# Softmax sums of the first five head pairs: GpSimd adds three key tiles to three others before TensorE sums them, and the written order is planned anew

## The chip, the cores and the metric

The kernel runs on one core of one Trainium2 chip. The metric is the device time of one launch in microseconds; three runs of the kernel before gave 902.53, 903.97 and 904.75 us, a median of 903.97.

## The reference

```python
q_pool = q.reshape(B, H, S // 2, 2, D).mean(axis=3)      # B=4, H=8, S=1152, D=64
scores = scale * q_pool @ k.T                            # 576 queries by 1152 keys, a head
attn = exp(scores - max(scores))
attn = attn / (sum(attn) + 1e-9)                         # the sum over 1152 keys
x = heads side by side (attn @ v)                        # 2304 tokens by 512
h = x @ w_in                                             # 512 by 2048
out = (h * clip(h + 3, 0, 6) / 6) @ w_out                # 2048 by 512
```

All data are float32.

## The kernel before, in words

Attention goes by 16 head pairs g, numbered batch by batch. The scores are kept transposed: keys on the 128 partitions (nine key tiles t), queries on the free axis, 288 of the 576 at a time (halves h = 0, 1). So a unit of work (g, h) holds two heads j, nine tiles each of 128x288, in one tile `s`. For each unit TensorE makes the score tiles (`scores`, step `mm`), ScalarE copies them to `s` (`keep`, step `cp`) and VectorE keeps a running maximum over the tiles (`most`, step `mx`). `fold`, `best` and `spread` (steps `s1` to `s3`) turn it into one maximum for each query, spread over the partitions. `lessen` (step `su`, L470) subtracts it from three key tiles at a time (128x864), on VectorE or, in the first part, on GpSimd (which then reads a copy `mb` that ScalarE makes of it). `expo` (step `ex`, L478) takes the exponential, again three tiles at a time. `values` (step `av`, L495) multiplies with V.

The denominators are made in two ways. The first five pairs (g below EARLY = 5, "the first part") use `sums_of_four` (step `o4`, L525 to L531): for each of nine key tiles and two heads a matmul with a stationary block of ones (32 columns), into four 32-row strips of one PSUM tile, 18 matmuls in a unit, each recorded as two instructions. `keep_sums` (`sc`) and `pick_sums` (`de`) then reduce the strips. The other eleven pairs ("late" in the code) use `total` (step `ad`, L480 to L488): GpSimd adds three key tiles to three others (n = 0), adds the last three (n = 1) and folds the three that are left (n = 2, 3) in a tile `d` of pool `dp`, which has two buffers.

Also in the first part the two weight matrices are converted (`load_raw`, `convert`, `save_w`): raw words are loaded in 32 pieces of 512 KB, go in seven steps through ScalarE, GpSimd and VectorE (the last one, step 6, L629, on GpSimd or VectorE) and are written back to DRAM. A step named `second` waits for all maxima of the first five pairs and for 24 of the conversions; then PSUM is divided anew. Only after it do the late pairs' scores start, and the gated MLP (`do_layer` L183, `do_project` L216), which goes over chunks of 256 tokens between the attention steps. The last 768 tokens come in a loop of their own after attention.

The order of the instructions on each engine is written out by `Order.run`, a list scheduler on the host: every step has a place (a number, smaller goes first), costs for each engine that may run it, steps that it needs, and buffers that it takes and frees. Whenever an engine is free in the plan, it takes the ready step with the smallest place; a third number in a cost is added to the place for that engine (BIAS). Places come from the constants at the top: PER (distance between pairs, in the first part and later), AT and ATL (offsets of the steps of a pair, early and late), START and SLOPE (the MLP's chunks), LAG and MLP (steps inside a chunk), CONV and CSTEP (conversions). The engines run the list in order, so an instruction that waits holds up what stands behind it on its engine. The steps of the change are `o4` (L791), `ad` (L767 to L771), and the constants of L22 to L33.

Of the kernel before, what the change touches and what calls it, by code (L numbers as in the profile page):

```python
# [18 lines left out]


SBUFS = 3
START = (94.79, 128.23, 169.33, 204.1, 247.91, 270.62)  # L22
SLOPE = (2.19, 3.02, 2.72, 2.51, 1.78, 3.47)
LAG, MLP = 9.42, (2.56, -1.5, 4.75, 1.71)
CONV, CSTEP = 27.2, (39.17, 25.6)
NEAR = 5
EARLY, FCV = 5, 12
CVB = 1
BIAS = (-3.16, 165.7, 1.3, -2.73, 8.4, 2.65)
CUT = 8  # L30
PER = (18.24, 19.02)
AT = (1.82, 3.28, -1.17, 8.45, 1.17, 16.24, 17.65, 6.2, 8.03, -0.11, 4.3, 2.83, -21.04, 27.48)
ATL = (0.23, 5.42, -4.41, 15.94, 13.8, 18.37, 11.77, 34.99, -2.44, 15.27, 4.54, 6.0, -6.43, -6.01)  # L33
TAIL = 768


class Order:
# [9 lines left out]
    def add(self, key, place, cost, fn, needs=(), takes=(), frees=()):  # L47
        assert key not in self.key, key
        self.key[key] = len(self.steps)
        self.steps.append((place, cost, fn, tuple(needs), tuple(takes), tuple(frees)))  # L50
# [76 lines left out]
def pooled_attention_then_gated_mlp(ctx, tc, q, k, v, w_in, w_out, out):  # L127
    nc = tc.nc
    B, H, S, D = q.shape
    DM, DFF = w_in.shape  # L130
    P = 128
    KT = S // P
    KC = 3
# [70 lines left out]
    def hidden(pool, ps, xs, w, n):  # L204
        layer(ps, xs, w)
        r6 = relu(pool, ps, n)
        gate(r6, r6, ps)
        gh = upper(pool, r6, n)
        return gh, lower(pool, r6, gh, n)
# [46 lines left out]
    with ExitStack() as a:  # L256
# [12 lines left out]
        HQ = SQ // NH  # L269
        TQ = QT // NH  # L270
        ones = const.tile([P, 32], F32, name="ones")
# [12 lines left out]
        ps_t, s_t, m_t, st_t, d_t, av_t, x_t, xo_t, q_t = {}, {}, {}, {}, {}, {}, {}, {}, {}  # L284
# [40 lines left out]
        def bank(g):  # L325
            return ("v",) if g < NEAR else ("s",)
# [197 lines left out]

        def sums_of_four(eng, g, h):  # L525
            ps = d_t["p", g, h] = ps_av.tile([P, 512], F32, tag="av", name="psr")
            for t in range(KT):
                for i in (t % 2, 2 + t % 2):
                    nc.tensor.matmul(
                        ps[32 * i:32 * (i + 1), 0:HQ], ones[:, 0:32], s_t[g, h][:, i // 2, t, :], start=(t < 2), stop=(t > KT - 3)  # L530
                    )  # L531

        def keep_sums(eng, g, h):
            d_t["s", g, h] = sm.tile([P, HQ], F32, tag="sc", name="sc", bufs=1)
# [147 lines left out]
        add = od.add  # L682
        MOVE = {"ACT": (360, 440), "DVE": (480, 555, 1.5)}

        def place(g):
            return PER[0] * min(g, EARLY) + PER[1] * max(g - EARLY, 0)


        for g in range(NG):
            lead = place(g - 1)  # L690
            at = ATL if g >= EARLY else AT
            UNIT = PER[g >= EARLY] / 4
            early = g == 0
# [7 lines left out]
            late = g >= EARLY  # L701
            for c in C3 if late else range(2):
                n = 3 if late or c else 6
# [3 lines left out]
                cost = (750, 855) if late else (90 + 92 * n, 190 + 92 * n)  # L707
                add(("kh", g, c), z + 2 + c, {"ACT": cost} if late else {"ACT": cost, "DVE": (68 + 133 * n, 150 + 133 * n, BIAS[2])},
                    partial(keep_k, g=g, c=c),
# [3 lines left out]
            for h in range(NH if late else 1):  # L713
                z = place(g) + 2 * UNIT * h - at[1]
                for j in range(2 if late else 1):
# [3 lines left out]
                        [("pq", g, 1)] + [("second",)] * (g == NEAR) + before, bank(g), ("qp",) if h == NH - 1 and end or not late else ())  # L719
                    add(("qh", g, h, j), z, {"ACT": (300, 400)} if late else {"ACT": (505, 605), "DVE": (668, 750, BIAS[3])}, partial(keep_q, g=g, h=h, j=j),  # L720
                        [("tq", g, h, j)], () if j else ("q",), () if late else bank(g))
                    if late:
                        add(("ql", g, h, j), z, {"DVE": (375, 450)}, partial(keep_q, g=g, h=h, j=j), [("qh", g, h, j)], (), bank(g))
            for h in range(NH):
                for j in range(2):
# [36 lines left out]
                    for c in C3:  # L762
                        add(("su", u, c), z + at[3] + c, {"DVE": (970, 1045)} if late else {"DVE": (970, 1045), "POOL": (2000, 2050, BIAS[0])}, partial(lessen, u=u, c=c),
                            [("s3", u) if late else ("sb", u)] + ([("su", u, c - 1)] if c and late else []), (),
                            (("st",) if c == 2 else ()) if late else (("st", u, 3), ("mb", u, 3)))
                        add(("ex", u, c), z + at[3] + 1 + c, {"ACT": (831, 930)}, partial(expo, u=u, c=c), [("su", u, c)])
                    for n in range(4 if late else 0):  # L767
                        cost = 2000 if n < 2 else 765
                        add(("ad", u, n), z + at[4] + 1.5 * n, {"POOL": (cost, cost + 50)}, partial(total, u=u, n=n),
                            [("ex", u, c) for c in (range(2) if n == 0 else (2,) if n == 1 else ())] + ([("ad", u, n - 1)] if n else []),  # L770
                            () if n else ("d",), (("S", u[:2], 3),) if n == 1 else ())  # L771
# [5 lines left out]
                n = len(cuts) - 2  # L777
# [6 lines left out]
                ya = y + n  # L784
                z += at[6]
                add(("ev", g, h), ya, {"ACT": (296, 376), "DVE": (370, 450, BIAS[4])}, partial(take_v, g=g, h=h), [("av", g, h, n)], ("x",), ("av",))
                if late:
                    add(("de", g, h), z, {"PE": (510, 730)}, partial(sums, g=g, h=h),
                        [("dj", (g, h, j)) for j in range(2)] + [("av", g, h, n)], ("av",), ("dh",))
                else:  # L790
                    add(("o4", g, h), ya, {"PE": (2700, 2900)}, partial(sums_of_four, g=g, h=h), [("av", g, h, n)], ("av",), ("S",))  # L791
                    add(("sc", g, h), ya, {"ACT": (300, 400)}, partial(keep_sums, g=g, h=h), [("o4", g, h)])
                    add(("de", g, h), ya, {"PE": (510, 730)}, partial(pick_sums, g=g, h=h), [("sc", g, h)])
                add(("rc", g, h), z, {"DVE": (200, 280)}, partial(recip, g=g, h=h), [("de", g, h)])
                add(("rw", g, h), z, {"ACT": (370, 450), "POOL": (980, 1000, BIAS[5])}, partial(widen, g=g, h=h), [("rc", g, h)])
                add(("qu", g, h), z, {"PE": (250, 470)}, partial(quotient, g=g, h=h), [("rw", g, h)])
# [5 lines left out]
        COSTS = ({"ACT": (580, 680)}, {"POOL": (660, 670)}, {"DVE": (500, 570)}, {"DVE": (630, 700)}, {"DVE": (630, 700)},  # L802
                 {"POOL": (690, 720), "ACT": (600, 700, 3)}, {"POOL": (1280, 1300), "DVE": (640, 720, BIAS[1])})
        for f in range(NFC):
# [20 lines left out]
        for m in range(NFC * len(chunks)):  # L825
            c, f = divmod(m, NFC)
            z = START[c] + SLOPE[c] * f
            if f == 0:
# [37 lines left out]
    with ExitStack() as a:  # L866
# [11 lines left out]
        for step in range(NFC + lag):  # L878
            for n, f in ((0, step), (1, step - lag)):
                if 0 <= f < NFC:  # L880
                    w = parts[n][1]
                    g = hidden(gt if n else gp, ph[n].tile([P, DM], F32, tag="h", name="ph")[:, 0:w], xs[n], w_t[f, 0], w)
                    pend.append((n, g, f))
                    if len(pend) > 2:
                        n, g, f = pend.pop(0)
# [36 lines left out]
```

## Time and profile before

| | |
|---|---|
| median of three runs | 903.97 us |
| the profiled execution's own time | 904.39 us |
| its span, first to last instruction | 902.5 us |
| TensorE (PE) busy | 863.0 us, 96% |
| VectorE (DVE) busy | 638.4 us, 71% |
| ScalarE (ACT) busy | 618.4 us, 69% |
| GpSimd (POOL) busy | 523.4 us, 58% |
| mean granted TensorE clock | 0.987 |

The shares are averages over two stages that differ. Until about 185 us the first five pairs and the conversions run; from about 260 us on, TensorE has hardly a gap. Rows of windows (busy time of every engine in a stretch) show that better than the totals. A timeline row gives start, duration, engine, line, operation, operands and count, and in brackets the idle time of that engine before it with what ended it.

### The profile page before, as it was taken

The numbers are of one execution on the slowest core, as the hardware profiler recorded it, in microseconds if no ns is written. First come the engines' busy times: TensorE is split into PE (matmuls) and PEld (weight loads), VectorE is DVE, ScalarE is ACT, GpSimd is POOL, SyncE is SP. The second block draws the span as 40 slices with busy tenths as digits, with TensorE's granted clock in tenths as the row PEclk, the third lists the DMA queues.
The fourth block names the chain that finished last, engine by engine and source line by source line (L and its number), as shares of the span: only waits on it lengthen the run. The fifth ranks groups of instructions, "written<-read, shape, count | busy, mean of one in ns | idle before, by whom it ended". The sixth has DMA issues, their size and how long they took to land.

```text
span 902.5 us, 16987 instructions
## 1 busy us (share of the span) xinstructions
PE 863.0 (96%) x5976; PEld 671.9 (74%) x5976; DVE 638.4 (71%) x1196; ACT 618.4 (69%) x1320; POOL 523.4 (58%) x474
## 2 busy tenths in 40 slices
PE   4889989989999999999999999999999999999997
PEld 3445445457778887889888888888888877888886
DVE  5879989887898888777877777787876761322222
ACT  4878888875778888878777787787876763222222
POOL 2556747444567888867686977677885695000000
PEclk9889999999999999999999999999999999999999
DMA  9978576469988777769686787787678658534433
GB/s 261 277 225 257 201 232 218 156 205 303 323 273 276 222 234 207 245 218 320 213 246 214 223 280 236 266 273 250 221 262 273 198 189 282 181 121 135 138 96 93
DMA packets 113396, 204.00 MB, mean 226 GB/s; under 512 B 44448, under 2 KB 68000, under 8 KB 113312
## 3 DMA queue, kind: packets, MB, share of 16 engines
q1 hardware_dynamic: 112624, 201.55, 70.1%
q10 hardware_dynamic: 688, 1.38, 0.5%
q8 instruction: 47, 0.77, 0.4%
q14 instruction: 37, 0.30, 0.1%
HBM read 171.97 MB, written 30.93 MB: 225 GB/s over the span
## 4 chain that ended last, share of the span: by engine, by line
PE 75%; DMA 7%; DVE 7%; ACT 5%; issue 3%; POOL 2%; SPq 0%; DVEq 0%; ACTq 0%; POOLq 0%
PE ph L183 21%; PE po L216 16%; PE pav L495 12%; PE pqk L408 12%; PE pt L216 5%; DVE m L426 3%; DMA raw<-in_moe_w_in_dram 2%; DMA raw<-in_moe_w_out_dram 2%; PE pst L465 2%; ACT s L310 2%; PE pt L382 1%; DMA qr<-in_q_dram 1%; ACT s L478 1%; DMA w_d<-scratch 1%; PE psr L521 1%
## 5 line engine op out<-in xcount | busy, mean ns | idle before, releaser
L470 DVE TENSOR_TENSOR s<-s,pst 128x864 f32<-128x864 f32 x168 | 173.8, 1047 | 32.6 <-PE pst L465 27.4
L478 ACT ACTIVATE s<-s 128x864 f32<-128x864 f32 x192 | 176.7, 933 | 24.6 <-DVE s L470 22.6
L183 PE MATMUL ph<-mxmxh,w 128*128 128x256 f32 x896 | 181.0, 285 | 0.0
L426 DVE TENSOR_TENSOR m<-pqk,m 128x288 f32<-128x288 f32 x308 | 139.6, 453 | 38.2 <-ACT s L310 27.0
L495 PE MATMUL pav<-s,vr 128*64 128x288 f32 x1152 | 156.6, 417 | 0.0
L310 ACT COPY s<-pqk 128x288 f32<-128x288 f32 x396 | 145.9, 400 | 14.3 <-PE pqk L408 10.8
L183 PEld LDWEIGHTS ph<-mxmxh,w 128*128 128x128 f32 x896 | 146.5, 190 | 2.2 <-issue 0.9
L216 PE MATMUL po<-w,gh 128*128 128x512 f32 x448 | 139.3, 392 | 0.0
L188 ACT ACTIVATE r<-ph,three 128x256 f32<-128x256 f32 (+1 forms) x128 | 64.1, 501 | 102.1 <-PE ph L183 98.2
L183 PE MATMUL ph<-mxmxl,w 128*128 128x256 f32 x448 | 126.4, 282 | 0.0
L408 PE MATMUL pqk<-qh,kT 128*128 128x288 f32 x396 | 124.2, 327 | 2.2 <-DVE m L426 1.0
L488 POOL TENSOR_TENSOR d<-s 128x864 f32<-128x864 f32 x44 | 90.1, 2048 | 58.1 <-ACT s L478 55.2
L495 PEld LDWEIGHTS pav<-s,vr 128*64 128x64 f32 x1152 | 78.1, 138 | 59.1 <-issue 11.1
L192 DVE SCALAR_TENSOR_TENSOR r<-r,ph 128x256 f32<-128x256 f32 (+1 forms) x128 | 57.5, 449 | 90.2 <-ACT r L188 89.7
L408 PE MATMUL pqk<-ql,kT 128*128 128x288 f32 x396 | 111.6, 294 | 0.0
L201 POOL TENSOR_TENSOR gl<-r,gh 128x256 fp32r<-128x256 f32 x96 | 70.9, 738 | 52.1 <-ACT gh L196 34.1
L216 PEld LDWEIGHTS po<-w,gh 128*128 128x128 f32 x448 | 84.3, 188 | 14.5
L216 PE MATMUL po<-w,gl 128*128 128x512 f32 x224 | 90.0, 402 | 1.5 <-DMA w<-w_d 1.5
L488 POOL TENSOR_TENSOR d<-d,s 128x864 f32<-128x864 f32 x44 | 90.3, 2051 | 0.6
L408 PEld LDWEIGHTS pqk<-qh,kT 128*128 128x128 f32 x396 | 74.6, 188 | 17.8 <-DVE m L426 5.2
L183 PEld LDWEIGHTS ph<-mxmxl,w 128*128 128x128 f32 x448 | 85.2, 190 | 0.8
L196 ACT CAST gh<-r 128x256 fp32r<-128x256 f32 (+1 forms) x128 | 55.7, 435 | 39.3 <-DVE r L192 26.7
(97 smaller groups left out, 1500.7 us busy)
## 6 DMA issues: line engine op xcount, KB each, us to landing
w<-w_d SPq DMA_DIRECT2D x224, 512.0 KB, 5.0
w_d<-scratch SPq DMA_DIRECT2D x32, 512.0 KB, 5.5
kr<-in_k_dram SPq DMA_DIRECT2D x32, 288.0 KB, 5.0
vr<-in_v_dram SPq DMA_DIRECT2D x16, 576.0 KB, 4.0
qr<-in_q_dram SPq DMA_DIRECT2D x15, 576.0 KB, 6.8
raw<-in_moe_w_in_dram SPq DMA_DIRECT2D x16, 512.0 KB, 5.3
raw<-in_moe_w_out_dram SPq DMA_DIRECT2D x16, 512.0 KB, 5.1
xh_d<-xh SPq DMA_DIRECT2D x32, 144.0 KB, 4.8
```

Source lines behind the costliest of these rows:

```text
L183: nc.tensor.matmul(ps, w[:, wi, cs], x[:, c, :], start=(m == 0), stop=(m == 3 * NCC - 1))
L188: nc.scalar.activation(out=r6, in_=ps, func=AF.Relu, bias=three)
L192: nc.vector.scalar_tensor_tensor(out=out, in0=r6, scalar=6.0, in1=ps, op0=ALU.min, op1=ALU.mult)
L201: on.tensor_tensor(out=gl, in0=r6, in1=gh.bitcast(F32), op=ALU.subtract)
L216: nc.tensor.matmul(o, g[:, ts], w[:, wi, :], start=(f == 0 and n == 0), stop=(f == NFC - 1 and n == 2))
L310: nc.scalar.copy(out=out, in_=in_)
L408: nc.tensor.matmul(ps[:, 0:HQ], kT[g][:, j, t, :], w[:, j, :], start=(m == 0), stop=(m == 1))
L426: nc.vector.tensor_tensor(out=m, in0=ps, in1=s0 if t == 1 else m, op=ALU.max)
L470: by[eng].tensor_tensor(out=s, in0=s, in1=m.unsqueeze(1).to_broadcast([P, KC, HQ]), op=ALU.subtract)
L478: nc.scalar.activation(out=s, in_=s, func=AF.Exp, scale=SCALE)
L488: by[eng].tensor_tensor(out=out, in0=x, in1=y, op=ALU.add)
L495: nc.tensor.matmul(av_t[g, h][j * D:(j + 1) * D, :], vr_t[g][:, j, t, :], s_t[g, h][:, j, t, :], start=(t == 0), stop=(t == KT - 1),)
```

## The change

`sums_of_four` now reads, for each head, a tile `d` that holds key tiles 0 to 2 plus key tiles 3 to 5, and the key tiles 6 to 8 of `s`: six tiles and 12 matmuls in place of nine and 18. `d` is made by the existing `total` with n = 0, one addition of 128x864 on GpSimd for each head, now also in the first part: 20 additions in all. The step `o4` waits for both of them and frees their two buffers, and its planned cost goes from 2.7 to 1.68 us. All constants of the planner except NEAR, EARLY, FCV, CVB, CUT, SBUFS and TAIL have new values, so the order of the instructions changes on every engine and on the DMA queue. The late pairs' computation is the same.

```diff
-START = (94.79, 128.23, 169.33, 204.1, 247.91, 270.62)
-SLOPE = (2.19, 3.02, 2.72, 2.51, 1.78, 3.47)
-LAG, MLP = 9.42, (2.56, -1.5, 4.75, 1.71)
-CONV, CSTEP = 27.2, (39.17, 25.6)
+START = (91.67, 120.91, 188.71, 198.91, 254.62, 284.32)
+SLOPE = (2.44, 4.32, 2.56, 3.51, 1.77, 3.22)
+LAG, MLP = 8.19, (2.71, 0.27, 8.03, 3.88)
+CONV, CSTEP = 10.02, (25.78, 34.41)
...
-BIAS = (-3.16, 165.7, 1.3, -2.73, 8.4, 2.65)
+BIAS = (-6.31, 220.17, 2.08, -2.07, 9.51, 5.35)
...
-PER = (18.24, 19.02)
-AT = (1.82, 3.28, -1.17, 8.45, 1.17, 16.24, 17.65, 6.2, 8.03, -0.11, 4.3, 2.83, -21.04, 27.48)
-ATL = (0.23, 5.42, -4.41, 15.94, 13.8, 18.37, 11.77, 34.99, -2.44, 15.27, 4.54, 6.0, -6.43, -6.01)
+PER = (18.47, 19.5)
+AT = (1.74, 2.54, -1.77, 8.3, 4.0, 15.83, 15.85, 5.03, 24.13, 1.63, 1.27, 2.12, -19.56, 48.55)
+ATL = (-0.24, 8.24, -2.07, 47.21, -0.55, 12.89, 18.9, 47.71, -5.11, 7.9, 1.16, 2.51, -0.41, -4.26)
...
         def sums_of_four(eng, g, h):
             ps = d_t["p", g, h] = ps_av.tile([P, 512], F32, tag="av", name="psr")
-            for t in range(KT):
+            d = [d_t.pop((g, h, j)) for j in range(2)]
+            for t in range(2 * KC):
                 for i in (t % 2, 2 + t % 2):
-                    nc.tensor.matmul(
-                        ps[32 * i:32 * (i + 1), 0:HQ], ones[:, 0:32], s_t[g, h][:, i // 2, t, :], start=(t < 2), stop=(t > KT - 3)
-                    )
+                    x = d[i // 2][:, t] if t < KC else s_t[g, h][:, i // 2, KC + t, :]
+                    nc.tensor.matmul(ps[32 * i:32 * (i + 1), 0:HQ], ones[:, 0:32], x, start=(t < 2), stop=(t > 2 * KC - 3))
...
-                    for n in range(4 if late else 0):
+                    for n in range(4 if late else 1):
                         cost = 2000 if n < 2 else 765
                         add(("ad", u, n), z + at[4] + 1.5 * n, {"POOL": (cost, cost + 50)}, partial(total, u=u, n=n),
...
-                    add(("o4", g, h), ya, {"PE": (2700, 2900)}, partial(sums_of_four, g=g, h=h), [("av", g, h, n)], ("av",), ("S",))
+                    add(("o4", g, h), ya, {"PE": (1680, 1880)}, partial(sums_of_four, g=g, h=h), [("av", g, h, n)] + [("ad", (g, h, j), 0) for j in range(2)], ("av",), ("S", "d", "d"))
```

## Rows read from the trace of the kernel before

**Rows 1.** The page, parts 1 and 2: engine busy times, and TensorE's granted clock.

```profile
PE 863.0 (96%) x5976; PEld 671.9 (74%) x5976; DVE 638.4 (71%) x1196; ACT 618.4 (69%) x1320; POOL 523.4 (58%) x474
...
PEclk9889999999999999999999999999999999999999
```

**Rows 2.** Windows by stage: length, engines' busy us (instructions), clock, DMA share, GB/s.

```profile
13.00:185.00 172.00, 152.43 (x1157) 80.98 (x1155) 154.43 (x237) 137.69 (x236) 98.92 (x84) 0.95 0.74 231
...
215.00:260.00 45.00, 43.46 (x310) 34.10 (x310) 39.64 (x76) 30.66 (x75) 27.29 (x29) 1.00 0.93 302
260.00:758.00 498.00, 497.35 (x3590) 416.82 (x3590) 379.19 (x756) 386.26 (x890) 379.29 (x338) 1.00 0.75 241
758.00:902.50 144.50, 137.54 (x695) 116.55 (x693) 38.74 (x69) 38.25 (x71) 1.55 (x2) 0.99 0.43 139
```

**Rows 3.** Groups by line, 0 to 240 us: the sums with ones.

```profile
L529 PE MATMUL psr<-s,ones 128*32 128x288 f32 x360 | 26.2, 409 | 1.6 <-ACT x L310 1.2 <-DVE x L312 0.4
```

**Rows 4.** TensorE's timeline: the last three of the ten `o4` steps.

```profile
182.96 2.62 PE L529 MATMUL psr<-s,ones 128*32 128x288 f32 x36 [0.71 <-ACT x L310]
...
204.21 2.62 PE L529 MATMUL psr<-s,ones 128*32 128x288 f32 x36
...
232.87 2.62 PE L529 MATMUL psr<-s,ones 128*32 128x288 f32 x36
```

**Rows 5.** The chain of waits, 0 to 185 us: start, us, what.

```profile
51.16 7.34 DMA raw<-in_moe_w_out_dram
...
149.79 2.57 PE psr L529 x36
...
166.78 2.55 PE psr L529 x36
```

**Rows 6.** GpSimd's addition of three tiles to three, late pairs: ns min/median/max.

```profile
L488 POOL TENSOR_TENSOR d<-s x44: 2017/2051/2088, 241.1 to 742.9; 128x864 f32<-128x864 f32 x44
```

**Rows 7.** ScalarE's timeline: the last exponentials before the `o4` at 182.96.

```profile
173.48 0.92 ACT L478 ACTIVATE s<-s 128x864 f32<-128x864 f32 x1
174.82 0.93 ACT L478 ACTIVATE s<-s 128x864 f32<-128x864 f32 x1
```

**Rows 8.** `lessen` on its two engines, ns, then both in a window (DVE, POOL).

```profile
L470 DVE TENSOR_TENSOR s<-s,pst x168: 1008/1047/1056, 31.1 to 741.3; 128x864 f32<-128x864 f32 x168
L470 POOL TENSOR_TENSOR s<-s,mb x24: 2015/2028/2054, 30.2 to 196.4; 128x864 f32<-128x864 f32 x24
...
13.00:185.00 172.00, 33.00 (x32) 44.44 (x22) 0.95 0.74 231
```

**Rows 9.** Step 6 of the conversions on VectorE, ns; one of them, and GpSimd beside it.

```profile
L629 DVE TENSOR_TENSOR scratch<-scratch x13: 681/693/2571, 19.4 to 274.8; 128x512 fp32r<-128x512 f32 x13
...
110.49 1.25 DVE L629 TENSOR_TENSOR scratch<-scratch 128x512 fp32r<-128x512 f32 x1
...
110.18 2.42 POOL L320 TENSOR_TENSOR qp<-qr 96x384 f32<-96x384 f32 x2
```

**Rows 10.** TensorE's timeline: the three longest pauses between 13 and 185 us.

```profile
17.63 1.30 PE L348 MATMUL pv<-ident,kr 128*128 128x128 f32 x9 [2.35 <-DMA kr<-in_k_dram]
...
35.08 1.93 PE L404 MATMUL pv<-qh,kT 64*128 64x288 f32 x8 [1.96 <-DVE m L426]
...
60.52 0.74 PE L559 MATMUL psr<-ident,rw 96*128 96x96 f32 x3 [2.45 <-ACT rw L310]
```

**Rows 11.** ScalarE's timeline at the third pause.

```profile
58.58 0.66 ACT L605 ACTIVATE scratch<-raw 128x512 f32<-128x512 f32 x1 [1.94 <-DMA raw<-in_moe_w_out_dram]
```

**Rows 12.** Windows of 5 us around the pauses, columns as in rows 2.

```profile
20.00:25.00 5.00, 4.43 (x18) 2.37 (x16) 4.10 (x7) 2.18 (x5) 0.61 (x1) 0.50 1.04 348
...
35.00:40.00 5.00, 4.92 (x23) 2.81 (x23) 4.36 (x7) 4.49 (x9) 4.25 (x4) 0.66 0.81 239
...
60.00:65.00 5.00, 4.48 (x19) 2.20 (x19) 4.87 (x8) 4.36 (x8) 4.85 (x4) 0.50 0.72 216
```

**Rows 13.** TensorE's first layer of the MLP, both parts: ns, first and last start.

```profile
L183 PE MATMUL ph<-mxmxh,w x896: 274/283/388, 188.2 to 880.5; 128*128 128x256 f32 x180
```

## The prediction

> **What bounds the kernel now.** I read the page's totals first, then windows by stage, then the chain of waits and the timelines of single engines inside the first stage. The totals say 96% TensorE [rows 1], which would make every matmul removed a gain. The windows [rows 2] break that up. From 260 to 758 us TensorE is busy 497.35 of 498 us: nothing but TensorE's work sets the time there. From 13 to 185 us it is busy 152.4 of 172 us, VectorE 154.4 of 172: two engines at nine tenths, and neither full. The changed matmuls lie mostly in that stage. GpSimd, which gets new work, is busy 98.9 of 172 us there. In the chain of waits of that stage [rows 5] only two of its eight sums with ones appear; the rest of the chain hops between VectorE's maxima, ScalarE's copies and loads of the raw weights. So the first stage ends when a string of small hand-overs ends, not when one engine is done.
>
> **Matmuls removed.** The ten sums with ones take 26.2 us of TensorE in all [rows 3], 2.62 us each [rows 4], for 18 matmuls: 0.146 us a matmul. Six of them go in each: 0.87 us, 8.7 us over ten. Their worth depends on where they stand.
> - Two, at 204.21 and 232.87 us [rows 4], stand after the late scores and the MLP have begun. TensorE is busy 43.46 of 45 us from 215 to 260 [rows 2], and all its later work follows. I count them in full: -1.75 us.
> - Eight lie before 185 us, 7.0 us together. Where VectorE ends the step, TensorE then only waits longer. Bounds: 0 to -7.0. I take the two that the chain names [rows 5]: -1.75 us.
>
> **Additions put in.** GpSimd gets 20 additions of 128x864; the same operation takes 2.05 us for the late pairs [rows 6], so 41 us, of which 16, 32.8 us, fall before 185 us. That makes 131.7 of 172 us, 77%. From 260 to 758 us GpSimd is busy 379.3 of 498 us, 76% [rows 2]: a share at which it keeps up here, hardly below the new one. Two consequences have to be priced.
>
> First, the wait: `o4` now needs both additions. Behind a waiting `o4` on TensorE stand the next pair's score matmuls, and for them wait ScalarE's copies and then VectorE's maxima. Before the `o4` at 182.96 [rows 4] the last exponential ended at 175.75 us [rows 7], 7.2 us earlier, while `values` ran; the additions need only the second of each head's three exponentials, which comes earlier still. Two additions with one subtraction of 2.03 us in front [rows 8] are 6.1 us. So the cover holds. If it is gone, two additions and two subtractions make 8.2 us, 1.0 us late, 10 us over ten units. Bounds 0 to +10; I take 0. ScalarE's work and the two `d` buffers, used by nothing else until the late pairs, add nothing of their own.
>
> Second, displacement: 22 subtractions run on GpSimd between 13 and 185 us and 32 on VectorE [rows 8]. One that goes back costs VectorE 1.05 us, and VectorE is the engine with the least room. Going the other way, the changed bias (-6.31 for -3.16) makes GpSimd bid for them earlier; the 40 us that it would have left hold 19 of them, -20 us of VectorE. Half of the 22 going back is +11.5 us. With 77% against the 76% row I take 0: about as many stay.
>
> **An aside on the shared port.** VectorE's last conversion step, which reads two SBUF tensors, has a median of 0.69 us, but took 1.25 us beside a GpSimd instruction, and that one was stretched as well, to 2.42 us for two; the longest record is 2.57 us [rows 9]. The Trainium skill, "GPSIMD Engine Reference", section Specifications, says that GpSimd shares its SBUF interfaces with VectorE and contends with VectorE instructions in a two-port mode or with two SBUF inputs; the trace agrees for this step, and it speaks against more GpSimd work. It leaves out the instructions that read PSUM, and indeed the subtraction on VectorE stays between 1.01 and 1.06 us [rows 8]. By the rule, 13 such steps colliding each time at 0.56 us would cost 7.3 us; by the rows' median they mostly miss each other, and the sum carries nothing for it.
>
> **The new order.** Every step's place changes, so the DMA issues on the SP queue move too: loads of K, Q and V of each pair, 64 loads and stores of conversion, and the MLP's weights. What this can give or take is bounded by the pauses. TensorE's three longest between 13 and 185 us are 2.35, 1.96 and 2.45 us [rows 10]; the third began because ScalarE stood in its queue before a late raw load [rows 11], whose transfer the chain shows as 7.34 us [rows 5]. Behind each, the granted clock fell to its lower level, 1.2 of 2.4 GHz, for a time: 0.50, 0.66 and 0.50 in the following 5 us windows [rows 12], that is, half of 4.43 and 4.48 us and a third of 4.92 us were lost, 2.2, 2.2 and 1.7 us. Pauses with their slow stretches are 4.6, 3.6 and 4.7 us, 12.9 together. Bounds: -12.9 if all go, +12.9 if as many come. I take one average pause saved without its slow stretch, since VectorE kept busy for 4.87 us in the slow window from 60 to 65 us: -2.25 us. An order with shorter raw-load waits early is as likely to have them, since conversions move forward relative to attention (CSTEP 25.78 for 39.17). Where a stall goes, the next thing late is VectorE itself, at 154.4 us of work.
> From 260 to 758 us the idle time is 0.65 us [rows 2]; a new order can only add there. I take as much again: +0.65 us. The tail's loop after 758 us keeps its instructions; the 7 us of idle time in that window may shift either way, 0.
>
> **Sum.** -1.75 - 1.75 - 2.25 + 0.65 = -5.1 us. The profiled execution took 904.39 us (span 902.5 and 1.9 around it), so 899.3; it lies 0.42 above the median of the three runs, so 898.9 us is the forecast. 0.3% is 2.7 us, about what a measurement can tell from no change: faster means below 901.3, slower above 906.7.
>
> **Rivals.**
> - *Hidden in the first stage* (0.20): VectorE's 154.4 us and the raw loads keep their rhythm, the eight sums before 185 us save nothing and the pauses stay. For it: only two of eight on the chain, VectorE busier than TensorE. Against: VectorE still idles 17.6 us. Left are -1.75 + 0.65: 902.9 us.
> - *GpSimd hands work back* (0.16), the slower side: the additions push subtractions to VectorE between 13 and 185 us, at 1.05 us each. Four returning (4.2 - 1.1) already pass 2.7 us, so it decides from there; at seven, 7.35 - 1.1 = +6.25 us, 910.2 us. For it: VectorE at 90%, GpSimd at 77% with work that arrives in bursts. Against: the stage at 76% that loses nothing, and the new bias.
> - *TensorE paces worse* (0.08): with 7 us less to do, it pauses more often, and each pause of about 2.4 us is followed by a stretch at the lower clock. Two more at 4.7 us and none saved: +9.4 - 1.1, 912.3 us. For it: each of the three long pauses was followed by a lower clock [rows 10, 12]. Against: the new order may close pauses as well as open them. The Trainium skill, "TensorE: Matmul & The Clock Gate", section Part 1: The HAM clock gate, says that the throttled state is the default and only activity releases it; rows 12 agree, and by it less matmul work in a stage with gaps is a risk, not a free gain.
> - *The pauses go* (0.16): the three pauses and their slow stretches vanish: -12.9 - 1.75 - 1.75 = -16.4, 887.6 us at the best. For it: the third came from one late load only, and the stage's engines all have 17 us to spare. Against: VectorE and TensorE are both at nine tenths.
> - That the change doesn't do what it says I hold for out of the question: six fewer matmuls and one more addition a head are in the code of every unit.
>
> **How the numbers follow.** Forecast 0.40, with its own range of 894.5 to 901.3 us; hidden 0.20 is the chance of the same; GpSimd and clock together 0.24 are slower; forecast and pauses 0.56 faster. The range of 889 to 909 us leaves out the better half of the pauses' case (0.08) and half of the two slower cases (0.12).
>
> **What would show it.** 240 instructions of L529 with 17.5 us in place of 360 with 26.2 us. 20 more GpSimd rows of about 2.05 us. The MLP starting some 3 to 4 us earlier than at 188.2 us [rows 13]. Subtractions on GpSimd about 22 before that point; fewer than 18 would mean that work was handed back. TensorE's busy time from there on full as before. TensorE waiting for GpSimd's `d` in front of L529 would show my cover wrong; a first stage of the old length with more idle TensorE would show the hidden case; more 5 us windows at a clock of 0.5 the pacing case.

## The result: slower by 1.4%

The changed kernel takes 917.84 us (median of six runs) beside 905.34 us for the kernel before on the same chips: a ratio of 1.0141, 95% interval 1.0116 to 1.0167. The forecast was 898.9 us in a range of 889 to 909; it missed in direction and size. The profiled execution took 919.72 us, span 917.9.

Windows by stage of the changed kernel, columns as in [rows 2]:

```profile
13.00:185.00 172.00, 147.48 (x1033) 77.64 (x1035) 157.20 (x232) 133.81 (x227) 119.31 (x89) 0.93 0.70 214
185.00:215.00 30.00, 24.72 (x201) 16.91 (x198) 25.18 (x46) 23.19 (x48) 20.69 (x18) 0.94 0.81 258
215.00:260.00 45.00, 42.79 (x303) 33.94 (x303) 38.53 (x79) 31.90 (x76) 24.87 (x25) 1.00 0.97 316
260.00:758.00 498.00, 488.09 (x3509) 410.56 (x3506) 379.57 (x757) 380.22 (x884) 370.66 (x332) 1.00 0.75 237
```

Against [rows 2], TensorE idles 24.5 us for 19.6 between 13 and 185 us, and 9.9 for 0.65 between 260 and 758 us. Over the whole span its busy time is 861.0 for 863.0 us, its idle time 56.9 for 39.5: the loss is idle time, most of it in two stages. The busy time hides a second one: ten sums at 1.66 us for 2.62 (below) should have taken 9.6 us off it, and it fell by 2.0, so other matmuls took longer (the granted clock is 0.93 for 0.95 in the first window). VectorE is busy 157.2 us in that window, 2.8 more than before, although TensorE has no more to do there: 1033 records for 1157, of which 168 and 286 are the sums.

The MLP's first layer and the sums with ones, from the views that gave [rows 13] and [rows 5]:

```profile
L183 PE MATMUL ph<-mxmxh,w x896: 274/283/516, 203.9 to 896.2; 128*128 128x256 f32 x180
...
170.97 1.66 PE psr L531 x24
```

A sum now takes 1.66 us for 2.62 [rows 4]; that part did what it says. But the MLP starts at 203.9 us, 15.7 us later than before [rows 13].

The next view groups by line, 0 to 215 us, of the changed kernel: step 6 of the conversions on VectorE and on GpSimd, GpSimd's subtractions and its additions.

```profile
L470 POOL TENSOR_TENSOR s<-s,mb 128x864 f32<-128x864 f32 x21 | 42.8, 2046 | 20.6 <-ACT mb L310 20.5
L488 POOL TENSOR_TENSOR d<-s 128x864 f32<-128x864 f32 x20 | 41.6, 2098 | 0.2 <-PE psr L531 0.2
...
L629 POOL TENSOR_TENSOR scratch<-scratch 128x512 fp32r<-128x512 f32 x13 | 16.7, 1283 | 5.7 <-PE psr L531 4.0 <-ACT scratch L310 1.5
L629 DVE TENSOR_TENSOR scratch<-scratch 128x512 fp32r<-128x512 f32 x12 | 15.9, 1333 | 0.7 <-ACT scratch L310 0.6
```

All 24 subtractions but three stayed on GpSimd. The odd row is the last: 12 steps on VectorE take 15.9 us, 1.33 us each, where the median before is 0.69 [rows 9]. 12 x 0.69 is 8.3, so 7.6 us of VectorE's time are stretch. The timelines of VectorE and GpSimd show where it comes from, in three places of the changed kernel:

```profile
112.20 1.89 DVE L629 TENSOR_TENSOR scratch<-scratch 128x512 fp32r<-128x512 f32 x1
...
153.86 4.36 DVE L629 TENSOR_TENSOR scratch<-scratch 128x512 fp32r<-128x512 f32 x2
...
259.87 3.17 DVE L629 TENSOR_TENSOR scratch<-scratch 128x512 fp32r<-128x512 f32 x1
```

```profile
111.53 2.02 POOL L488 TENSOR_TENSOR d<-s 128x864 f32<-128x864 f32 x1
...
151.46 3.99 POOL L488 TENSOR_TENSOR d<-s 128x864 f32<-128x864 f32 x2
155.41 2.26 POOL L323 TENSOR_TENSOR qp<-qr 96x768 f32<-96x768 f32 x1
...
259.59 0.72 POOL L201 TENSOR_TENSOR gl<-r,gh 128x256 fp32r<-128x256 f32 x1
260.27 0.78 POOL L488 TENSOR_TENSOR d<-d 128x288 f32<-128x288 f32 x1
261.02 0.72 POOL L201 TENSOR_TENSOR gl<-r,gh 128x256 fp32r<-128x256 f32 x1
261.70 0.78 POOL L488 TENSOR_TENSOR d<-d 128x288 f32<-128x288 f32 x1
```

Each long step lies on an addition of the change or on a train of GpSimd instructions, and ends 0.54 to 0.56 us after one of them has ended (114.09 after 113.55, 158.22 after 157.67, 263.04 after 262.48). TensorE stands behind it in the same two stages (its timeline):

```profile
158.74 0.46 PE L465 MATMUL pst<-ident,mq 96*128 96x96 f32 x3 [2.79 <-DVE mq L453]
...
263.67 0.51 PE L448 MATMUL pst<-ident,pm 128*96 128x128 f32 x3 [2.91 <-DVE pm L442]
```

Two theories came out of this. P (port): the additions meet VectorE's two-input steps on a shared way to SBUF. O (order): the new order costs by itself. Q (queue), a third, came with the first experiments: the additions only make GpSimd's queue longer, and others wait for what stands behind them.

### The profile page after: what moved, and what is told of

Its sections match the earlier page's. It is cut to its first block, busy times and chain, and to the rows that moved or that the text cites. A ratio compares the mean times of both kernels' runs of the same rounds, so it can differ in the third digit from the quotient of the medians.

```text
span 917.9 us, 16731 instructions
## 1 busy us (share of the span) xinstructions
PE 861.0 (94%) x5856; PEld 670.7 (73%) x5856; DVE 645.8 (70%) x1202; ACT 619.1 (67%) x1323; POOL 551.8 (60%) x485
## 4 chain that ended last, share of the span: by engine, by line
PE 69%; DVE 12%; DMA 7%; ACT 6%; issue 4%; POOL 1%; SPq 0%; DVEq 0%; ACTq 0%; POOLq 0%
PE ph L183 18%; PE po L216 14%; PE pav L495 13%; PE pqk L408 10%; PE pt L216 5%; DVE m L426 3%; DMA w<-w_d 3%; DVE s L470 3%; ACT s L310 2%; PE pv L404 2%; DVE kT L367 2%; PE pst L448 1%; PE pst L465 1%; DVE scratch L629 1%; ACT s L478 1%
## 5 line engine op out<-in xcount | busy, mean ns | idle before, releaser
L470 DVE TENSOR_TENSOR s<-s,pst 128x864 f32<-128x864 f32 x171 | 177.2, 1045 | 17.1 <-PE pst L465 14.1
L495 PE MATMUL pav<-s,vr 128*64 128x288 f32 x1152 | 159.5, 423 | 4.3 <-DVE x L563 4.3
L310 ACT COPY s<-pqk 128x288 f32<-128x288 f32 x396 | 148.0, 401 | 21.5 <-PE pqk L408 19.4
L488 POOL TENSOR_TENSOR d<-s 128x864 f32<-128x864 f32 x64 | 132.2, 2071 | 40.7 <-ACT s L478 32.7
L408 PE MATMUL pqk<-qh,kT 128*128 128x288 f32 x396 | 121.9, 321 | 3.0 <-DVE kT L367 2.1
L216 PEld LDWEIGHTS po<-w,gh 128*128 128x128 f32 x448 | 84.4, 188 | 14.5
L408 PEld LDWEIGHTS pqk<-ql,kT 128*128 128x128 f32 x396 | 75.1, 190 | 2.2
```

The lines of the kernel that those rows point to most:

```text
L216: nc.tensor.matmul(o, g[:, ts], w[:, wi, :], start=(f == 0 and n == 0), stop=(f == NFC - 1 and n == 2))
L310: nc.scalar.copy(out=out, in_=in_)
L408: nc.tensor.matmul(ps[:, 0:HQ], kT[g][:, j, t, :], w[:, j, :], start=(m == 0), stop=(m == 1))
L470: by[eng].tensor_tensor(out=s, in0=s, in1=m.unsqueeze(1).to_broadcast([P, KC, HQ]), op=ALU.subtract)
L488: by[eng].tensor_tensor(out=out, in0=x, in1=y, op=ALU.add)
L495: nc.tensor.matmul(av_t[g, h][j * D:(j + 1) * D, :], vr_t[g][:, j, t, :], s_t[g, h][:, j, t, :], start=(t == 0), stop=(t == KT - 1),)
```

## The experiments

Each ratio is to the kernel before, from runs on the same chip, with its 95% interval. e5 is one run and only its trace is read.

### The parts alone

**e1: the new order without the new work.**

```diff
 def total(eng, u, n):
+    if u[0] < EARLY: return
 def sums_of_four(...):
+    (the loop over nine key tiles of s_t, as before)
```

> The changed kernel's order of instructions on every engine, planned as there, but the sums of the first part are the old 18 matmuls and the 20 additions are not issued. Theory O (the new order itself is bad: ratio to before comes from pauses and transfers): 1.012 to 1.018, MLP's first layer still starting near 204 us, idle time of TensorE between 260 and 758 us still near 10 us. Theory P (the 20 additions on GpSimd meet VectorE's two-input conversion steps and lengthen them in the first stage): the first stage shortens by 8 us or more, MLP's first layer near 196 us or earlier, VectorE's conversion step back from 1.33 to about 0.8 us mean, ratio 1.005 or less, though with 8.7 us more of TensorE's work.

1.0060 (1.0043 to 1.0076); the MLP starts at 199.2 us. Two of its windows, and the one pause of TensorE of 1.9 us or more that is left between 13 and 185 us:

```profile
13.00:185.00 172.00, 156.45 (x1169) 83.17 (x1168) 155.22 (x241) 137.25 (x233) 86.67 (x74) 0.94 0.73 222
260.00:758.00 498.00, 490.51 (x3533) 411.12 (x3533) 374.34 (x751) 380.47 (x883) 376.26 (x337) 1.00 0.75 238
```

```profile
17.78 2.15 PE L348 MATMUL pv<-ident,kr 128*128 128x128 f32 x9 [2.31 <-DMA kr<-in_k_dram]
```

TensorE idles 7.5 us between 260 and 758 us: the new order brings most of that idle time itself. In the first stage it idles less than before, 15.6 us for 19.6. VectorE's step 6 is back at 766 ns mean. Neither theory alone: the order costs 0.6%, the work the rest.

**e2: the old order with the new work.** Each addition is issued behind the second of the two exponentials that it needs, as soon as a buffer of `d` is free; `sums_of_four` is that of the change.

```diff
 for fn, eng in [...] + od.run():
     fn(eng)
+    (an expo of c < 2, g < EARLY, the second of its head: pending.append(u))
+    (a sums_of_four: free_d += 2)
+    while pending and free_d:
+        free_d -= 1
+        total("POOL", pending.pop(0), 0)
```

> The order of the kernel before, kept as it is on every engine, with the additions put on GpSimd behind the second exponential of their head (later where both buffers are taken) and the sums of 12 matmuls. Theory O (the new order is to blame): 0.994 to 0.999, the gain of the matmuls after 200 us and some of those before. Theory P (the additions lengthen VectorE's conversion steps and the subtractions that wait on GpSimd): 1.003 to 1.010, first stage 4 to 10 us longer, conversion steps on VectorE at 1.1 us mean or more.

1.0202 (1.0186 to 1.0219), worse than the change itself. With two buffers, the order planned for the work is better for it than the old one (with four it is not: e14, below), and the work is dear.

**e3: fewer matmuls, nothing else.**

```diff
-for t in range(KT):
+for n, t in enumerate((0, 1, 2, 6, 7, 8)):
```

> The order of the kernel before, the sums made of key tiles 0 to 2 and 6 to 8 alone (tiles 3 to 5 are left out of the denominators), no additions: the matmuls' removal by itself. My sum said -1.75 after 185 us and -1.75 of 7.0 before, ratio 0.996. If the first stage is bound by VectorE and the hand-overs alone: 0.998. If TensorE binds it throughout: 0.990.

1.0037 (1.0012 to 1.0061): no gain at all, rather a loss. In its profiled run the MLP starts at 187.1 us, 1.1 us earlier, and ends 1.0 us later than before. Its windows around the start of the late pairs (first fence), beside those of the kernel before (second):

```profile
185.00:190.00 5.00, 4.10 (x36) 3.69 (x36) 2.81 (x5) 1.64 (x4) 3.01 (x3) 1.00 0.86 270
190.00:195.00 5.00, 3.44 (x15) 1.69 (x15) 4.25 (x8) 4.88 (x10) 0.13 (x2) 0.60 0.68 176
195.00:200.00 5.00, 5.00 (x30) 3.14 (x29) 4.10 (x8) 2.78 (x7) 3.49 (x3) 0.72 0.17 59
```

```profile
190.00:195.00 5.00, 3.39 (x18) 1.46 (x16) 3.93 (x7) 4.87 (x10) 0.53 (x1) 0.76 0.79 211
195.00:200.00 5.00, 5.00 (x38) 3.79 (x36) 4.91 (x9) 4.08 (x9) 3.53 (x3) 0.90 0.18 61
```

TensorE's pause in front of the slow stretch, in e3 and before:

```profile
191.56 0.71 PE L382 MATMUL pt<-ident,qp 96*128 96x96 f32 x3 [2.47 <-DVE kT L367]
```

```profile
191.90 0.44 PE L382 MATMUL pt<-ident,qp 96*128 96x96 f32 x3 [1.61 <-DVE kT L367]
```

TensorE comes earlier and waits longer for VectorE, 2.47 us for 1.61; then follows a clock of 0.60 and 0.72 for 0.76 and 0.90 (part of the time at 1.2 GHz, the rest at 2.4): TensorE does 45 instructions for 56 in those 10 us. From 13 to 185 us the clock is 0.92 for 0.95; the sums with ones take 7.1 us less there (13.30 for 20.37), TensorE's busy time falls by 1.6. In this run, what the matmuls leave is paid back in slow ones.

**e4: the additions alone.** The edit of e2 without the new sums.

> The order of the kernel before with its 18 matmuls and all maths unchanged, plus the 20 additions on GpSimd, whose result nothing uses: the additions by themselves. My sum said 0, ratio 1.000. Theory P: 1.006 to 1.012, the first stage longer by 5 to 11 us; whether by VectorE's stretched conversion steps or by subtractions that wait behind the additions on GpSimd is read from VectorE's L629 durations and from ScalarE's and VectorE's waits for GpSimd.

1.0141 (1.0119 to 1.0164), with nothing else changed. The MLP starts at 204.0 us. Ten steps 6 on VectorE in the first 245 us take 14.5 us, 1.45 each. The longest, on VectorE's timeline, and the two additions on GpSimd's:

```profile
120.02 4.76 DVE L629 TENSOR_TENSOR scratch<-scratch 128x512 fp32r<-128x512 f32 x1
```

```profile
120.25 3.99 POOL L488 TENSOR_TENSOR d<-s 128x864 f32<-128x864 f32 x2
```

But the waits of that run name a second way as well, VectorE in its own queue before a conversion's step 2, for GpSimd's step 1, which stands behind additions (the row of e4, then of the kernel before):

```profile
DVE pv L613 <- POOL scratch L607: 8.9, 6, 3.0
```

```profile
DVE pv L613 <- POOL scratch L607: 1.5, 3, 0.7
```

### The shared way to SBUF

**e5: the collision by itself.**

```diff
 (behind the end of the kernel)
+pool(6); dve(6)          # GpSimd alone, then VectorE alone
+pool(24) beside dve(6)   # dve(n): n adds SBUF+SBUF, n adds PSUM+SBUF, n copies in SBUF, 128x512
```

> The kernel before, with a block behind its end: six GpSimd additions of 128x864 alone; then on VectorE alone six 128x512 additions of two SBUF tensors, six of a PSUM and an SBUF tensor, six copies within SBUF; then the same 18 on VectorE beside 24 GpSimd additions. Its total time is not compared. Theory P: the two-SBUF additions go from 0.69 to over 1.5 us beside GpSimd, those with a PSUM input stay as they are, and the GpSimd additions beside the first kind are stretched or hold VectorE off until they end. Rival (the lengthening in the traces is VectorE waiting for its inputs, not the port): all durations alike in both blocks.

VectorE's timeline, first alone, then beside GpSimd (the copies were scheduled between the additions), and GpSimd's (of the 24 additions the last 12 once more by themselves):

```profile
915.51 0.69 DVE L913 TENSOR_TENSOR vt<-vu,vv 128x512 f32<-128x512 f32 x1
916.12 0.42 DVE L917 COPY vc<-vu 128x512 f32<-128x512 f32 x1
...
921.14 4.31 DVE L915 TENSOR_TENSOR vt<-vp,vv 128x512 f32<-128x512 f32 x6
...
932.06 2.48 DVE L913 TENSOR_TENSOR vt<-vu,vv 128x512 f32<-128x512 f32 x1
934.47 2.22 DVE L917 COPY vc<-vu 128x512 f32<-128x512 f32 x1
...
954.81 4.30 DVE L915 TENSOR_TENSOR vt<-vp,vv 128x512 f32<-128x512 f32 x6
```

```profile
902.35 12.40 POOL L909 TENSOR_TENSOR gz<-gx,gy 128x864 f32<-128x864 f32 x6 [145.18 <-DVE gy L904]
...
926.94 52.70 POOL L909 TENSOR_TENSOR gz<-gx,gy 128x864 f32<-128x864 f32 x24
...
954.68 24.96 POOL L909 TENSOR_TENSOR gz<-gx,gy 128x864 f32<-128x864 f32 x12
```

0.69 becomes 2.48 us, somewhat more than a GpSimd addition; the additions with a PSUM input stay at 0.72; copies within SBUF go from 0.42 to 2.22. The rival (late inputs) is out: nothing here waits for data. GpSimd's own additions take 2.07 us alone, 2.31 us while they meet the first two kinds (the first 12, 27.74 us) and 2.08 us after.

**e6 and e7: the additions without the two-input step, and the control.**

```diff
 elif step == 6:
+    if eng == "DVE": nc.vector.memset(w[:, 1, :], 0.0)
```

> The old order with the 20 additions (as e4), but where step 6 of a conversion runs on VectorE it is a memset of the lower half instead of a subtraction of two SBUF tensors (the lower halves of those weight pieces are left out). Theory P (port): most of the cost of the additions goes, ratio 1.004 or less against 1.014 in e4; e7 is its control. Theory Q (the additions stand in GpSimd's queue ahead of conversion steps 1 and 5 and of subtractions, for which VectorE and ScalarE then wait in their own queues): still 1.009 or more, with VectorE's wait for GpSimd's L607 at 6 us or more.

> Control: the kernel before with the same memset in place of step 6 on VectorE (lower halves of those weight pieces left out), no additions. Ten steps in the first stage lose 0.1 to 0.2 us each: ratio 0.997 to 1.000. If it falls below 0.995, the port costs the kernel before already.

e6: 1.0074 (1.0055 to 1.0094); e7: 0.9970 (0.9951 to 0.9989). In e6 the additions still cost 1.0% over their control, 1.4% in e4. So the port makes 0.4 of the 1.4% in the old order, which is barely clear of the noise. Theory Q would be the rest: VectorE's wait for GpSimd's L607 is 9.8 us in e6.

**e8: the changed kernel without it**, same edit.

> The changed kernel with the memset in place of step 6 on VectorE (lower halves of those weight pieces left out). Its 12 such steps in the first stage are 15.9 us, 1.33 us each for 0.69 alone. Theory P: ratio to before falls from 1.014 to 1.006 or less, the level of the new order without the new work (e1). Theory Q: 1.010 or more.

1.0028 (1.0013 to 1.0043), the MLP at 194.5 us: 1.1% of the change's 1.4% are gone. 0.3% of that the control gains too, which leaves 0.8% for the port, some 7 us (about 4 to 11 with the three intervals). Up to 0.1% of it is the shorter instruction: the change has 18 such steps, the kernel before 13. The 7.6 us read from the row of L629 lie in that range, but are no second proof: e4 has the same stretch (14.5 us for ten steps of 0.69), and there the port is worth 0.4%. And 1.0028 / 0.9970 = 1.0058 is e1's 1.0060: without the port, the new work costs nothing measurable in the order that was planned with it, if the memset gains as much in the new order as in the old (e1 with it was not run). Theory P holds for the changed kernel, beside O.

### GpSimd's queue and the buffers

**e9: e6 with additions a third as long.**

```diff
+if u[0] < EARLY: out, x, y = out[:, 0], x[:, 0], y[:, 0]
```

> As e6 (old order, additions, memset for step 6 on VectorE; lower halves of those weight pieces left out), but each of the 20 unused additions is of 128x288 in place of 128x864, 0.8 for 2.05 us. Theory Q (what e6 still costs over its control e7, 1.0%, is GpSimd's queue: conversion steps and subtractions that stand behind the additions): two thirds of it go, ratio 1.001 or less. Rival (it is the wait of GpSimd for the exponential at the head of its queue, not the length): 1.005 or more.

0.9983 (0.9962 to 1.0005), 0.1% over the control where e6 had 1.0%. The length of the additions in the queue is what costs in the old order; Q holds there.

**e14 and e17: e2 with four buffers, then also without the two-input step.**

```diff
-free_d = 2                     +free_d = 4
-dp.tile(..., tag="d")          +dp.tile(..., tag="d", bufs=4)
```

> As e2 (old order, additions and 12 matmuls, full result; 1.020), with four buffers for the added tiles in place of two. If the 0.6% by which e2 is slower than e4 (additions without the new sums) comes from GpSimd standing at the head of its queue until the sums free a buffer: 1.014 or less, GpSimd's wait for the sums gone. If it comes from TensorE's pauses alone: 1.018 or more.

> As e14 (old order, additions, 12 matmuls, four buffers; 1.0074), with the memset for step 6 on VectorE (lower halves of those weight pieces left out); e7 (0.997) is the control. If the port is what is left of e14's cost: 1.000 or less. If GpSimd's fuller queue costs by itself: 1.003 to 1.006, as e6 against e9 has it.

e14: 1.0074 (1.0053 to 1.0095); e17: 1.0069 (1.0041 to 1.0097). GpSimd's wait for the sums, 7.3 us in e2, is gone in e14, with 1.3%. That is not the buffers alone: with four of them the additions also stand earlier in the queue, and step 6 on VectorE is at 0.96 us mean for 1.09 in e2. All the work of the change in the old order is then half as dear as the change itself. With the step gone as well (e17) nothing more is won, though the control gains 0.3% by that: some 1.0% stays, as in e6, but not shown to be the same 1.0%, since GpSimd now stands 11.1 us (e14) before additions whose exponentials are not done yet, for 0.8 in e4.

**e16: the changed kernel with four buffers**, its order kept.

> The changed kernel, its order kept on every engine, full result, with four buffers for the added tiles in place of two. GpSimd's wait for the sums at the head of its queue is 4.2 us in the profiled run of the changed kernel, in one place. If that wait costs what it lasts: ratio 1.010. If it is covered: 1.013 to 1.015.

1.0113 (1.0086 to 1.0139), an interval that overlaps that of the change. But the wait is still there with four buffers, so it was not for a buffer. GpSimd's timeline in the change and in e16, and ScalarE's in the change:

```profile
188.79 1.28 POOL L629 TENSOR_TENSOR scratch<-scratch 128x512 fp32r<-128x512 f32 x1 [3.98 <-PE psr L531]
```

```profile
189.43 1.28 POOL L629 TENSOR_TENSOR scratch<-scratch 128x512 fp32r<-128x512 f32 x1 [3.98 <-PE psr L531]
```

```profile
188.04 0.62 ACT L310 CAST scratch<-scratch 128x512 fp32r<-128x512 f32 x1 [0.24 <-DVE scratch L622]
```

What waits is a conversion's step 6. The view names the sums, which end at about that time too; but the step's input, step 5 on ScalarE, ends 0.13 us before it in the change (188.66) and in e16 alike. Four buffers take away only the other 0.2 us, so e16 tests next to nothing.

### Step 6 moved to GpSimd

**e10, in the kernel before, and e11, in the changed one.**

```diff
 elif step == 6:
-    by[eng].tensor_tensor(...)
+    nc.gpsimd.tensor_tensor(...)
```

> The kernel before in its own order, full result, with the 13 conversion steps 6 that ran on VectorE moved to GpSimd at the same place (1.28 us each there for 0.97 mean on VectorE). If the port cost is what e7 saved (0.3%): 0.997 to 1.000. If GpSimd's queue is as dear as theory Q has it (13 x 1.28 = 17 us put into it against 41 us of additions that cost 1.0%): 1.001 to 1.004.

> The changed kernel in its own order, full result, with the 18 conversion steps 6 of VectorE moved to GpSimd at the same place. The port's part (1.1%, e8) goes, 18 x 1.28 = 23 us of GpSimd come, and GpSimd is then busy some 80% of the first stage. Theory P alone: 1.003 as e8. With Q: 1.005 to 1.012.

e10: 1.0002 (0.9981 to 1.0022), the same. e11: 1.0091 (1.0060 to 1.0122), better than the change by half a per cent, but still behind the kernel before, and in the range that Q gave: a fuller queue of GpSimd may cost in the new order as well, which no run here tests by itself. No version with the full result beats the kernel before.

### The order's two parts, and the matmuls in the new order

**e12, e13: the old code with the first or the second part's constants new; e15: e1 with the edit of e3.**

```diff
 e12: AT, BIAS, PER[0], CONV, CSTEP[0] new
 e13: START, SLOPE, LAG, MLP, ATL, PER[1], CSTEP[1] new
```

> The kernel before (18 matmuls, no additions) with the new constants of the first part alone (AT, the first of PER, CONV, the first of CSTEP, BIAS), those of the second part old. e1 gave 1.006 with the MLP starting 11 us later and 7 us more of idle TensorE after 260 us. If the first part's new order costs: 1.005 or more, MLP starting near 199 us, hardly any idle time after 260 us. If the second part's: 0.998 to 1.002.

> The kernel before (18 matmuls, no additions) with the new constants of the second part alone (START, SLOPE, LAG, MLP, the second of PER and CSTEP, ATL). If the new order's 0.6% (e1) all comes from the first part (e12: 0.64%): 0.998 to 1.002. If the second part's order costs too and the two overlap in e1 (MLP started later, work waiting for it): 1.003 to 1.008, with idle time of TensorE between 260 and 758 us of 5 us or more.

> The changed kernel's order without the additions (as e1, 1.006), with the sums of key tiles 0 to 2 and 6 to 8 alone (tiles 3 to 5 left out of the denominators): the removal by itself in the new order. By my sum it is worth 3.5 us, ratio 1.002. If the removed work only makes pauses with a lower clock, as in e3: 1.005 to 1.009.

e12: 1.0064 (1.0041 to 1.0088); e13: 1.0147 (1.0111 to 1.0183), and both together only 1.0060 in e1. Both leave TensorE idle between 260 and 758 us (4.8 and 6.6 us). The parts don't add up, and need not: the order of e1 was planned with the additions and the shorter sums in the plan, those of e12 and e13 with the old work, and the old work planned with all the new constants was not run. Which constants cost what stays open. e15: 1.0069 (1.0046 to 1.0092) for e1's 1.0060: no gain from the removed matmuls shows in the new order either, where the sum had 0.4%.

## Why the prediction was wrong

The trace of the kernel before had one collision of the kind that the change multiplies: VectorE's longest step 6 [rows 9] lies on an addition of 128x864 for a late pair, and ends 0.56 us after it (VectorE's timeline, then GpSimd's).

```profile
249.58 2.57 DVE L629 TENSOR_TENSOR scratch<-scratch 128x512 fp32r<-128x512 f32 x1
```

```profile
249.54 2.05 POOL L488 TENSOR_TENSOR d<-s 128x864 f32<-128x864 f32 x1
```

By its own steps:

- *"the sum carries nothing for it"*, of the shared port: the step that failed most, by a little. The mechanism was named and 7.3 us worked out for 13 collisions of 0.56 us; it was dropped because the median of 0.69 us [rows 9] said that they mostly miss. That median comes from steps before 185 us, where GpSimd had none of the additions; its subtractions there are as long, and the steps mostly missed them. The longest step, 2.57 us, was the collision itself. Measured: 0.8% by e8 and e7, some 7 us, and 7.6 us of stretch on the row. That 7.3 comes so close is luck: six of the 12 steps before 215 us were stretched, by up to 1.5 us each, and 7.3 was no bound. The Trainium skill, "GPSIMD Engine Reference", section Specifications, which says that GpSimd contends with VectorE instructions in a two-port mode or with two SBUF inputs, agrees with e5 in every kind, the copy included if that ran in a two-port mode.
- *"-2.25"* and *"+0.65"*, the new order: measured +0.6%, 5.4 us, by e1. What failed is the step from a pause saved to time saved. In e1 two of the three pauses [rows 10] fall below 1.9 us and the first stage has 4.0 us less idle time, and still the MLP starts 11 us later and the kernel is slower; why stays open. Between 260 and 758 us TensorE idles 7.5 us in e1 and 9.9 in the change, for 1.3 in my sum; 2.9 of the 9.9 are the port again, at 263.67 us. The change has four pauses of 1.9 us or more in the first stage; three of them begin in a stretched step or just behind it, and e8 has none.
- *"-1.75"* twice, the matmuls: no gain in e3 and e15, rather a loss in e3. The two after 200 us were to count in full because TensorE is full there; but the slow stretch before them is longer. This is the rival in which TensorE paces worse, right in kind, though not as a slowdown of 9 us. The Trainium skill, "TensorE: Matmul & The Clock Gate", section Part 1: The HAM clock gate, has the throttled state as the default that only activity releases; e3's windows agree (a clock of 0.60 behind the longer pause, 0.76 behind the shorter).
- *The additions, "I take 0"* twice. The cover held: among the changed kernel's waits between 13 and 210 us none of TensorE is for an addition. Displacement hardly came: 20 subtractions on GpSimd for 22 [rows 8] from 13 to 185 us, so the rival that put the cost there was wrong in mechanism, right in sign. The 76% row as a measure of what GpSimd bears was no good: in the old order the same additions cost 1.0% without the port (e6 over e7), and it is their length that costs (e9); in the order that was planned with them no such cost shows (e8 beside e1).
- *"the two buffers ... add nothing"*: for the change this held, since GpSimd waits 0.2 us for them there. In the old order it waits 7.3 us (e2).

Put together for the change: 0.6% order (e1), 0.8% port (e8 and e7), nothing for the matmuls: 1.4%, as measured. Against the sum of the prediction the port is off by some 7.4 us, the order by 7.0 and the matmuls by 3.5.

## What to carry to other kernels

Work moved to an engine with spare time is priced by what that engine shares: list the instructions that use the shared port while it runs, look up what lay beside each long record of them, and price the case in which they collide, not the median from a stage in which they had nothing of that kind to collide with. A matmul removed where TensorE already has gaps is worth nothing until a run shows it, since the gaps brought the slow clock here. A stage without idle time can only lose by a new order, and its loss has to be bounded by more than what stood idle before.

## What the runs showed of the hardware

A VectorE instruction with two SBUF inputs, or a copy within SBUF, that meets GpSimd additions takes somewhat longer than one of them: 2.48 us for 0.69 and 2.22 us for 0.42 (e5). In the kernels it can last across several GpSimd instructions, 4.76 us across two additions (e4) and 3.17 us across four short ones (the change, at 259.87 us), and the subtractions looked at end 0.54 to 0.56 us after one of those has ended. An addition with one input in PSUM takes 0.72 us in both cases. GpSimd gives up less: 2.31 us for an addition of 2.07.
